# Two-expert-layer kernel behind attention: value products of the odd heads spread over three steps, a one-column bias, gating factors in PSUM, one operand prepared earlier

## The chip, the cores and the metric

One core of one Trainium2 chip. The metric is the device time of one execution in microseconds, the median of several runs. In the text PE is TensorE, DVE is VectorE, ACT is ScalarE, POOL is GpSimd, and SP issues the DMAs.

## What is computed

The reference chains three parts, cut here to what matters.

```python
# attention: batch 2, heads 8, seq 576, head_dim 64, fp32
scores = scale * np.matmul(q, k.transpose(0, 1, 3, 2))
thresh = np.max(scores, axis=-1, keepdims=True) - tau
scores = np.where(scores >= thresh, scores, -1000000000.0)
attn = np.exp(scores - np.max(scores, axis=-1, keepdims=True))
attn = attn / (np.sum(attn, axis=-1, keepdims=True) + 1e-09)
attn_out = np.matmul(attn, v)          # -> x, 1152 x 512
# first expert layer: 8 experts, 512 -> 1024 -> 512
logits = x @ w_gate
P = np.exp(logits - logits.max())
for _ in range(8):
    P /= P.sum(1, keepdims=True) + 1e-09
    P /= P.sum(0, keepdims=True) + 1e-09
    P *= N / E
for e in range(E):
    out += P[:, e:e + 1] * (np.maximum(x @ w1[e], 0.0) @ w2[e])
# second expert layer: the same with 4 experts and p = domain_probs / row sum
```

## The kernel before, in words

**Stage 1, attention, with the first two experts as filling.** The queries of 128 rows by all 576 keys of a head are one unit. The units stand in a list, 72 of them, and `Attention.step` (L388) emits one step per unit as a software pipeline: in step `t` the scores of unit `t+2` are multiplied (`scores`, into one of two PSUM tiles `sc`), unit `t+1` gets its row maximum (`top`, L275), its bias and threshold (`line`, L279) and its exponential (`exp`, L283, on ACT), unit `t` is masked and summed (`mask`, L287, DVE), and normalised on POOL (`norm`, L297), unit `t-2` is transposed on PE (`turn`, L305 and L307) and copied out of PSUM on ACT (`hi`, L312 and L314). Each engine runs its instructions in the order in which they are emitted, so this list of calls sets the order on every queue.

The first 16 units, rows 0 to 255 of batch 0, are the "exact" ones: their probabilities stay in fp32 in one tile `e32` of 5 key blocks by 512 columns, the even head of a pair in columns 0 to 255, the odd head in 256 to 511. Their products with the values (`mix`, L340, written as `pv`) take five key blocks per head, and each block shows as two rows of PE. A group of products (one per head, tied to the head's last unit) is visited in three successive steps: as `c` when that unit is three steps old, as `z` at four, as `y` at five. `parts` (L327) says which of the five blocks are multiplied in which visit, and `out` (L351) splits the finished product into `xh` (ACT, L357) and `xl` (DVE, L358). The other 56 units use a split into high and low fp32r parts, with `lo` (L322, L325) on DVE; from there on PE also gets the work of experts 0 and 1 (`expert_fill`, L460 and L488) between the units. Weights are split into `wh` (ACT) and `wl` (POOL or DVE) as they arrive (`cook`).

`line` makes two numbers of a row's maximum in one DVE instruction on two columns, with a tile `lin` of four columns as its two tensor inputs:

```python
V.scalar_tensor_tensor(st[:, 1:3], lin[:, 0:2], st[:, 0:1], lin[:, 2:4], op0=ALU.mult, op1=ALU.subtract)
```

Column 1 of `st` is the bias of the exponential, column 2 the threshold of the mask.

**Gating.** `gate` (L703) makes the gating matrix `p1` with eight rounds of row and column scaling, on DVE (L731 to L741) with one small product on PE per round (L737, which sums over partitions into a PSUM bank). Row factors `rs` (128x9) and column factors `cs` (128x8) are SBUF tiles. It runs between the last fill work of stage 1. `bank()` hands out PSUM banks, eight at that time.

**Stage 2.** The expert layers are worked off as a list of halves. `layer1` (L842) multiplies seven operand combinations in the order `SLOTS`, each product continuing in a PSUM bank that is copied (`snap`, L890), added to by DVE (L895, L902, L909) and passed through `done` (L860 ACT, L861 DVE); `layer2` (L972) multiplies with the second weights (L989) and accumulates (L997). The operands are sums and differences of `x`, made by `sums` (L761): first DVE sums (L772 to L781), then high and low parts of them by `split` (L71 on ACT, L76 on DVE), three of which live in `xt` (`xth`, `xtl`), six tile parts in all. `sums` is a generator: `s1 = sums(1)` is stopped where it needs `xt`, whose memory comes free only when the fills are closed (L818). After that it is put at the head of the list `behind`, from which `tick` takes one piece at a time, once after each slot of `layer1`; `drain` takes the rest before the first slot that uses `xt` (`u == 6`).

Of the kernel before, what the change touches and what calls it, by code (L numbers as in the profile page):

```python
# [9 lines left out]
F32 = mybir.dt.float32  # L10
F32R = mybir.dt.float32r
AF = mybir.ActivationFunctionType
ALU = mybir.AluOpType
# [3 lines left out]
B, H, S, D = 2, 8, 576, 64  # L17
N, DM, F = 1152, 512, 1024
E1, E2 = 8, 4
P = 128  # L20
KT = DM // P
FT = F // P
NT = N // P
# [6 lines left out]
def attention_two_moe_kernel(ctx, tc, qP, kP, qT, kT, vp, tau, wg, w1, w1s, w2, dp, m2w1s, m2w2, out):  # L30
    nc = tc.nc
    V, A, G, T = nc.vector, nc.scalar, nc.gpsimd, nc.tensor
# [7 lines left out]
    cp = pool(ctx, "const")  # L40
# [14 lines left out]
    warm = cp.tile([P, 1], F32, name="warm")  # L55
    A.activation(warm, ones[:, 0:1], AF.Exp)
    esc = cp.tile([P, 1], F32, name="esc")
    lin = cp.tile([P, 4], F32, name="lin")
    on = cp.tile([P, 1], F32, name="on")
    wg_sb = cp.tile([P, KT, E1], F32, name="wg_sb")  # L60
    wg2 = cp.tile([P, KT, 2 * E1], F32R, name="wg2")
# [49 lines left out]
    class Attention:  # L111
# [164 lines left out]

        def line(self, u):
            st = u["st"]
            V.scalar_tensor_tensor(st[:, 1:3], lin[:, 0:2], st[:, 0:1], lin[:, 2:4], op0=ALU.mult, op1=ALU.subtract)  # L279

        def exp(self, u):
            ex = u["ex"] = self.pl.tile([P, 2, HS], F32, tag="ex", name="ex", bufs=4)
# [43 lines left out]

        def parts(self, hd):  # L327

            return ((0, 1, 2, 3, 4), (), ()) if hd["h"] % 2 else ((0,), (1, 2), (3, 4))

        def mix(self, g, part):
            hd, n, c = g["head"], g["n"], slice(g["c"], g["c"] + g["n"])
# [55 lines left out]
        def step(self, fill, side):  # L388

            us, t = self.units, self.t  # L390
            un = lambda i: us[i] if 0 <= i < len(us) else None
            self.load()
            nxt, a, d, x, c, z, y = (un(t + i) for i in (2, 1, 0, -2, -3, -4, -5))
            if x:
                self.turn(x)
            if d:
                self.mask(d)
            if a:
                self.top(a)
            if d:  # L400
                self.guard(d)
            if a:
                self.line(a)
            if d:
                self.norm(d)
            for part, u in enumerate((c, z, y)):
                for g in u["mix"] if u else ():
                    if g["head"]["exact"]:
                        self.mix(g, part)
            if x:  # L410
                self.hi(x)
            for u, late in ((z, False), (y, True)):
                for g in u["mix"] if u else ():
                    if late == (g["head"]["exact"] and g["head"]["h"] % 2 == 0):
                        self.out(g)
            fill(0, bool(c and c["mix"]))
            if a:
                self.exp(a)
            if x:
                self.lo(x)  # L420
            if nxt:
                self.scores(nxt)
            self.run(self.later)
            for g in c["mix"] if c else ():
                if not g["head"]["exact"]:
                    self.mix(g, 0)
            fill(1, bool(c and c["mix"] or z and z["mix"]))
            self.run(self.late)
            for w in self.work.pop(t, ()):
                w()  # L430
            side()
            self.t += 1
            return self.t < len(us) + 5
# [12 lines left out]
    def bank():  # L446
        return banks.tile([P, 512], F32, tag="mm", name="mm")
# [60 lines left out]
    with ExitStack() as att:  # L508
# [14 lines left out]
        at.plan()  # L523
        room = [2 * FT]
        at.load()
        G.memset(lin, 0.0)
        G.memset(lin[:, 1:2], 1.0)
        V.tensor_scalar(on, tau_sb, 0.0, None, op0=ALU.is_ge)
        V.tensor_scalar(esc, on, 0.125, None, op0=ALU.mult)
        V.tensor_scalar(lin[:, 0:1], on, -0.125, None, op0=ALU.mult)  # L530
        V.tensor_scalar(on, on, -BIG, BIG, op0=ALU.mult, op1=ALU.add)
        V.scalar_tensor_tensor(lin[:, 3:4], tau_sb, 8.0, on, op0=ALU.mult, op1=ALU.add)

        def side():
            if at.t >= -1:
# [140 lines left out]
    behind = []  # L676
# [26 lines left out]
    def gate():  # L703
# [21 lines left out]
        T.matmul(pn[:, 0:1], lhsT=ones[:1, :], rhs=gm[:1, 1:2], start=True, stop=True)  # L725
        V.tensor_scalar(gm[:, 2:3], pn[:, 0:1], -1.0, None, op0=ALU.mult)
        A.activation(p1, p1, AF.Exp, bias=gm[:, 2:3])
        rs = gp.tile([P, NT], F32, name="rs")
        cs = gp.tile([P, E1], F32, name="cs")
        for _ in range(8):  # L730
            V.tensor_reduce(rs, p1, axis=AX.X, op=ALU.add)  # L731
            V.tensor_scalar(rs, rs, 1e-9, None, op0=ALU.add)
# [92 lines left out]
    hp = pool(ctx, "hs", reuse_waits="tile")  # L825
    tp = pool(ctx, "temps", reuse_waits="tile")
    pending = [None, s1]
    behind += [s1, gt, sl]

    def begin(c, work):  # L830
        pending[c] = chain(pending[c] or (), work)
# [240 lines left out]
```

## Time and profile before

| | |
|---|---|
| median of 3 runs | 1394.73 us (1394.54 to 1398.56) |
| the profiled execution's own time | 1393.83 us |
| its span, first to last instruction | 1392.0 us |
| mean granted clock of TensorE over the span | 0.991 |
| POOL busy in the span | 662.0 us (48%) |
| ACT busy in the span | 560.9 us (40%) |

The span is 1.8 us shorter than the execution it belongs to, which holds the start and the end of the program too. A busy share is an average over stages with different limits, so the rows further down are taken stage by stage. In those rows a timeline line gives start, duration, engine, source line, operation, output <- inputs, and in brackets how long the engine sat idle before it and what ended that idle time. A line of a source view gives minimum, median and maximum duration in ns, and the first and last start.

### The profile page before, as it was taken

The page shows a single profiled execution, that of the slowest core. Times are in us where ns is not written, and L with a number is a line of the kernel's source. Part 1 is how long each engine was busy: PE and PEld are TensorE (multiplying, and loading weights), DVE is VectorE, ACT ScalarE, POOL GpSimd, SP SyncE. Part 2 cuts the span into 40 slices and gives each one's busy share as a digit, 9 for nine tenths or more (in the row PEclk, how much of TensorE's full clock was granted, in tenths as well). Part 3 has the DMA queues.
Part 4 walks back from the last instruction along what each step waited for, and adds up shares of the span by engine and source line. Part 5 has one row for each costly group of instructions (what it writes and reads, how often), then busy time and mean ns, then how long its engine had stood idle before and what let it go on. Part 6 is the DMA issues. An engine that isn't in the chain of part 4 may idle for free.

```text
span 1392.0 us, 21443 instructions
## 1 busy us (share of the span) xinstructions
PE 1331.3 (96%) x8089; PEld 1191.5 (86%) x8089; DVE 710.0 (51%) x1579; ACT 560.9 (40%) x1286; POOL 662.0 (48%) x792
## 2 busy tenths in 40 slices
PE   7788999999889999999999999999899999999998
PEld 4578898889779898988889898988788989888887
DVE  6799999555654333343434343435653434334343
ACT  5767677421444242333323242423442424233331
POOL 5766777351565354345335443542433543453330
PEclk9999999999999999999999999999999999999999
DMA  5522231010221111111111011101011101111101
GB/s 164 154 83 78 77 97 44 24 31 9 72 73 54 46 51 34 54 46 31 54 40 60 24 53 47 58 26 46 24 46 46 61 24 54 46 38 47 31 8 61
DMA packets 42055, 73.61 MB, mean 53 GB/s; under 512 B 5088, under 2 KB 10336, under 8 KB 41952
## 3 DMA queue, kind: packets, MB, share of 16 engines
q1 hardware_dynamic: 41664, 71.96, 17.2%
q8 instruction: 64, 1.05, 0.3%
q14 instruction: 39, 0.32, 0.1%
q10 hardware_dynamic: 288, 0.28, 0.1%
HBM read 69.86 MB, written 2.36 MB: 52 GB/s over the span
## 4 chain that ended last, share of the span: by engine, by line
PE 76%; DVE 14%; ACT 5%; issue 2%; POOL 2%; DMA 0%; DVEq 0%; ACTq 0%; POOLq 0%
PE mm L989 37%; PE mm L885 29%; PE mm L488 4%; DVE ex L287 2%; PE mm L460 2%; DVE st L275 2%; DVE st L279 1%; DVE etl L322 1%; DVE mm L895 1%; ACT wh L71 1%; ACT ex L283 1%; PE pv L340 1%; PE sc L270 1%; ACT hs L860 1%; DVE hs L861 1%
## 5 line engine op out<-in xcount | busy, mean ns | idle before, releaser
L989 PE MATMUL mm<-wh,hs 128*128 128x512 f32 x1344 | 433.2, 395 | 0.0
L76 POOL TENSOR_TENSOR wl<-raw,wh 128x512 fp32r<-128x512 f32 x154 | 200.0, 1304 | 396.6 <-ACT wh L71 379.7
L989 PEld LDWEIGHTS mm<-wh,hs 128*128 128x128 f32 x1344 | 252.3, 188 | 58.0 <-DVE hs L861 0.5
L997 DVE SCALAR_TENSOR_TENSOR acc<-mm,p,acc 128x512 f32<-128x512 f32 x181 | 135.7, 750 | 300.9 <-PE mm L989 300.9
L989 PE MATMUL mm<-wl,hs 128*128 128x512 f32 x672 | 264.5, 394 | 0.0
L890 ACT COPY s<-mm 128x288 f32<-128x288 f32 x84 | 33.7, 402 | 439.4 <-PE mm L885 439.3
L885 PE MATMUL mm<-xh,wl 128*128 128x288 f32 x672 | 147.9, 301 | 16.4 <-ACT u L890 14.3
L861 DVE SCALAR_TENSOR_TENSOR hs<-mm,hs 128x288 fp32r<-128x288 f32 x252 | 111.2, 455 | 86.9 <-ACT hs L860 86.9
L860 ACT ACTIVATE hs<-mm 128x288 fp32r<-128x288 f32 x252 | 98.5, 408 | 132.6 <-DVE mm L895 71.8
L989 PEld LDWEIGHTS mm<-wl,hs 128*128 128x128 f32 x672 | 126.4, 188 | 28.2 <-POOL wl L76 0.4
L885 PE MATMUL mm<-xl,wh 128*128 128x288 f32 x672 | 145.0, 297 | 0.0
L885 PE MATMUL mm<-xh,wh 128*128 128x288 f32 x672 | 144.8, 297 | 0.0
L885 PEld LDWEIGHTS mm<-xh,wl 128*128 128x128 f32 x672 | 110.7, 190 | 25.0 <-ACT u L890 15.7
L76 POOL TENSOR_TENSOR wl<-ws,wh 128x512 fp32r<-128x512 f32 x88 | 114.9, 1309 | 32.6 <-ACT wh L71 32.6
L885 PE MATMUL mm<-xth,wl 128*128 128x288 f32 x504 | 109.2, 298 | 1.7 <-ACT xth L71 1.7
L885 PE MATMUL mm<-xtl,wh 128*128 128x288 f32 x504 | 109.2, 298 | 1.5 <-DVE xtl L76 1.5
L885 PEld LDWEIGHTS mm<-xl,wh 128*128 128x128 f32 x672 | 109.0, 190 | 0.0
L885 PE MATMUL mm<-xth,wh 128*128 128x288 f32 x504 | 108.8, 297 | 0.0
L885 PEld LDWEIGHTS mm<-xh,wh 128*128 128x128 f32 x672 | 108.6, 190 | 0.0
L867 POOL TENSOR_SCALAR ht<-hs 128x128 fp32r<-128x128 f32 x168 | 49.7, 302 | 110.5 <-ACT hs L860 97.9
L71 ACT CAST wh<-raw 128x512 fp32r<-128x512 f32 x154 | 95.3, 619 | 2.2 <-DMA raw<-in_w 0.5
L885 PEld LDWEIGHTS mm<-xtl,wh 128*128 128x128 f32 x504 | 81.8, 190 | 2.0 <-DVE xtl L76 2.0
(167 smaller groups left out, 2383.3 us busy)
## 6 DMA issues: line engine op xcount, KB each, us to landing
raw<-in_w SPq DMA_DIRECT2D x88, 256.0 KB, 2.9
raw<-in_w1s SPq DMA_DIRECT2D x56, 256.0 KB, 2.7
raw<-in_m2w1s SPq DMA_DIRECT2D x32, 256.0 KB, 2.7
raw<-in_m2w SPq DMA_DIRECT2D x32, 256.0 KB, 2.9
kr<-in_kT SPq DMA_DIRECT2D x22, 288.0 KB, 2.9
vr<-in_vp SPq DMA_DIRECT2D x24, 160.0 KB, 2.4
qr<-in_qT SPq DMA_DIRECT2D x8, 288.0 KB, 2.8
out_y<-acc SPq DMA_DIRECT2D x8, 256.0 KB, 2.0
```

Of the source, the lines that this page charges most:

```text
L71: A.copy(hi, src)
L76: el.tensor_tensor(lo, src, f(hi), op=ALU.subtract)
L275: V.tensor_reduce(st[:, 0:1], u["sc"][:, :, :HS], axis=AX.XY, op=ALU.max)
L287: V.scalar_tensor_tensor(ex, u["sc"][:, :, :HS], st[:, 2:3], ex, op0=ALU.is_ge, op1=ALU.mult, accum_out=st[:, 3:4])
L488: T.matmul(py[:, :256], lhsT=x, rhs=a[:, c0:c0 + 256], start=i == 0, stop=i == 3 * FT - 1)
L860: A.activation(hh, src, AF.Relu)
L861: V.scalar_tensor_tensor(hl, src, 0.0, f(hh), op0=ALU.max, op1=ALU.subtract)
L867: G.tensor_scalar(tail[j][:, :, q:q + 32], f(side[s][j][:, :, 2 * P:]), 1.0, 1.0, op0=ALU.mult, op1=ALU.mult)
L885: T.matmul(m, lhsT=w[:, (2 * g + kt) * P:(2 * g + kt + 1) * P], rhs=operand(u, kt, lo), start=first and j == 0, stop=j == len(ops) - 1, sk ...
L890: A.copy(z[name], m)
L989: T.matmul(py, lhsT=hs[x][:, k, o:o + P], rhs=w, start=n == 0, stop=n == 3 * HF - 1)
L997: V.scalar_tensor_tensor(acc[t], py, s, acc[t], op0=ALU.mult, op1=ALU.add)
```

## The change

**Value products.** `parts` gave an odd head all five blocks in its first visit; now every exact head but the last one is spread as the even heads were: block 0, then blocks 1 and 2, then 3 and 4. The visits of one step are emitted in the order oldest first (`y`, `z`, `c`) instead of youngest first. The `out` of the odd heads moves to the third visit with it.

**Bias.** `line` becomes two DVE instructions of one column each, with one tensor input (`st`) and a per-partition scalar (`lin`, now two columns). Two POOL memsets of `lin` go.

**Gating factors.** `rs` and `cs` become slices of one PSUM bank, held as long as the gating runs.

**Operand preparation.** The rest of `s1` is emitted at once, ahead of the first `layer1`, instead of standing first in `behind`.

```diff
-    lin = cp.tile([P, 4], F32, name="lin")
+    lin = cp.tile([P, 2], F32, name="lin")
...
-            V.scalar_tensor_tensor(st[:, 1:3], lin[:, 0:2], st[:, 0:1], lin[:, 2:4], op0=ALU.mult, op1=ALU.subtract)
+            V.tensor_scalar(st[:, 1:2], st[:, 0:1], lin[:, 0:1], None, op0=ALU.mult)
+            V.tensor_scalar(st[:, 2:3], st[:, 0:1], lin[:, 1:2], None, op0=ALU.subtract)
...
-            return ((0, 1, 2, 3, 4), (), ()) if hd["h"] % 2 else ((0,), (1, 2), (3, 4))
+            return ((0, 1, 2, 3, 4), (), ()) if hd["h"] == H - 1 else ((0,), (1, 2), (3, 4))
...
-            for part, u in enumerate((c, z, y)):
+            for part, u in ((2, y), (1, z), (0, c)):
...
-                    if late == (g["head"]["exact"] and g["head"]["h"] % 2 == 0):
+                    if late == (g["head"]["exact"] and g["head"]["h"] < H - 1):
...
-        G.memset(lin, 0.0)
-        G.memset(lin[:, 1:2], 1.0)
...
-        rs = gp.tile([P, NT], F32, name="rs")
-        cs = gp.tile([P, E1], F32, name="cs")
+
+        norms = bank()
+        rs, cs = norms[:, :NT], norms[:, 16:16 + E1]
...
-    behind += [s1, gt, sl]
+    for _ in s1:
+        pass
+    behind += [gt, sl]
```

PE's queue in the exact stage, from the step in which the first odd head has its first visit, before (`pv` are the value products, `sc` the scores, `et` and `er` the transposes; L340 is `mix`):

```order
L307 MATMUL er<-ident,ex 64x128
L340 MATMUL pv<-e_125,vr 64x256 x7
L270 MATMUL sc<-kh,qs 128x288 x2
L270 MATMUL sc<-kl,qs 128x288 x2
L305 MATMUL et<-ident,ex 128x128 x4
L307 MATMUL er<-ident,ex 64x128
L270 MATMUL sc<-kh,qs 128x288 x2
L270 MATMUL sc<-kl,qs 128x288 x2
L305 MATMUL et<-ident,ex 128x128 x4
L307 MATMUL er<-ident,ex 64x128
L340 MATMUL pv<-e_125,vr 64x256
```

The same piece now (the lines of the file moved by one):

```order
L308 MATMUL er<-ident,ex 64x128
L341 MATMUL pv<-e_125,vr 64x256 x3
L270 MATMUL sc<-kh,qs 128x288 x2
L270 MATMUL sc<-kl,qs 128x288 x2
L306 MATMUL et<-ident,ex 128x128 x4
L308 MATMUL er<-ident,ex 64x128
L341 MATMUL pv<-e_125,vr 64x256 x2
L270 MATMUL sc<-kh,qs 128x288 x2
L270 MATMUL sc<-kl,qs 128x288 x2
L306 MATMUL et<-ident,ex 128x128 x4
L308 MATMUL er<-ident,ex 64x128
L341 MATMUL pv<-e_125,vr 64x256 x3
```

The blocks per step go from 7, 0, 1, 2 to 3, 2, 3, 2 (one row of this list is one block), and in the steps with three the two of the older head stand first.

ACT's queue where stage 2 begins, before (`acc` is the last copy of the fills, `s` and `u` are snaps of `layer1`, `xth` the six casts of the rest of `s1`, `wh` a weight):

```order
L493 COPY acc_3656<-mm 128x256 x2
L890 COPY s<-mm 128x288
L71 CAST xth<-xy 128x288
L890 COPY s<-mm 128x288
L71 CAST wh<-raw 128x512
L71 CAST xth<-xy 128x288
L860 ACTIVATE hs<-mm 128x288
L71 CAST xth<-xy 128x288
L860 ACTIVATE hs<-mm 128x288
L71 CAST wh<-raw 128x512
L71 CAST xth<-xy 128x288 x3
L890 COPY u<-mm 128x288 x2
```

And now:

```order
L494 COPY acc_3726<-mm 128x256 x2
L71 CAST xth<-xy 128x288 x6
L892 COPY s<-mm 128x288 x2
L71 CAST wh<-raw 128x512
L862 ACTIVATE hs<-mm 128x288 x2
L71 CAST wh<-raw 128x512
L892 COPY u<-mm 128x288 x2
```

The six casts moved ahead of the first snap, and on DVE the six `xtl` (L76) ahead of the first L895; PE's own order is unchanged there.

## Rows read from the trace of the kernel before

**Rows 1.** The page: busy time, share of the span and instructions of each engine.

```profile
PE 1331.3 (96%) x8089; PEld 1191.5 (86%) x8089; DVE 710.0 (51%) x1579; ACT 560.9 (40%) x1286; POOL 662.0 (48%) x792
```

**Rows 2.** Busy time by stretch: stretch, its length, busy time (instructions) of PE, PEld, DVE, ACT, POOL, then the granted TensorE clock, the DMA share and GB/s. The stretches are the exact units, the split units, the fills after them, the gating, the start of stage 2 and the steady part of stage 2.

```profile
28.00:77.00 49.00, 38.46 (x207) 23.85 (x205) 36.52 (x98) 34.02 (x66) 34.63 (x37) 1.00 0.49 141
77.00:228.00 151.00, 138.67 (x1046) 131.45 (x1044) 143.12 (x363) 110.48 (x215) 108.25 (x147) 0.99 0.28 81
228.00:293.00 65.00, 62.63 (x485) 60.12 (x484) 34.65 (x92) 30.38 (x68) 29.93 (x58) 1.00 0.08 25
293.00:313.00 20.00, 17.62 (x144) 17.07 (x144) 18.41 (x48) 5.88 (x14) 11.81 (x9) 1.00 0.11 27
352.00:372.00 20.00, 16.74 (x103) 15.26 (x103) 10.33 (x21) 10.76 (x28) 8.13 (x8) 0.91 0.19 59
480.00:1392.00 912.00, 896.32 (x5177) 800.84 (x5175) 372.94 (x748) 306.34 (x757) 380.95 (x413) 1.00 0.14 42
```

**Rows 3.** What PE waited for in 28 to 77 us: who waited for whom, us in total, times, longest.

```profile
PE sc L270 <- DVE ex L287: 9.1, 9, 1.4
PE et L305 <- DVE etl L322: 1.4, 2, 1.1
```

**Rows 4.** What ACT waited for in the same stretch, same columns.

```profile
ACT e L312 <- PE pv L340: 6.8, 3, 3.1
ACT ex L283 <- DVE st L295: 5.9, 7, 1.1
```

**Rows 5.** Timeline of the exact stage: the three copies `e` that waited for `pv`, one burst of `pv`, one step with two blocks of `pv`, and a wait of the scores.

```profile
31.61 0.59 ACT L312 COPY e<-et 128x512 f32<-128x512 f32 x1 [3.11 <-PE pv L340]
...
42.41 3.66 PE L340 MATMUL pv<-e,vr 128*64 128x256 f32 x14
...
45.59 0.59 ACT L312 COPY e<-et 128x512 f32<-128x512 f32 x1 [2.09 <-PE pv L340]
...
48.64 0.54 PE L270 MATMUL sc<-kh,qs 128*128 128x288 f32 x2 [1.31 <-DVE ex L287]
...
52.91 1.08 PE L340 MATMUL pv<-e,vr 128*64 128x256 f32 x4
...
59.44 0.59 ACT L312 COPY e<-et 128x512 f32<-128x512 f32 x1 [1.58 <-PE pv L340]
```

**Rows 6.** What PE waited for in 77 to 228 us, the longest in total (us in total, times, longest).

```profile
PE et L305 <- DVE etl L322: 10.3, 13, 1.9
```

**Rows 7.** The chain of work that ended last, shares of the stretch 77 to 228 us by line.

```profile
by line: DVE ex L287 16.6%; DVE st L275 14.2%; DVE st L279 11.8%; DVE etl L322 11.0%; PE mm L488 6.8%; DVE eth L325 4.6%; ACT ex L283 4.5%; DVE xf L369 4.3%; DVE hl L469 4.3%; issue 4.1%; POOL wl L98 2.4%; PE et L305 1.7%; POOL xl L76 1.6%;
```

**Rows 8.** Three DVE lines over the whole span: `line` (L279), the guard of the sum (L291) and the mask (L287), minimum, median and maximum ns.

```profile
L279 DVE SCALAR_TENSOR_TENSOR st<-lin,st x72: 220/472/1323, 6.9 to 251.8; 128x2 f32<-128x2 f32 x72
...
L291 DVE TENSOR_SCALAR st<-st x72: 133/143/154, 9.5 to 253.9; 128x1 f32<-128x1 f32 x72
...
L287 DVE SCALAR_TENSOR_TENSOR ex<-sc,st,ex x72: 799/817/820, 8.1 to 253.0; 128x576 f32<-128x576 f32 x72
```

**Rows 9.** Busy time of L279 alone in the exact and the split stretch (stretch, length, DVE busy and instructions, clock, DMA).

```profile
28.00:77.00 49.00, 7.39 (x14) 1.00 0.49 141
77.00:228.00 151.00, 24.34 (x43) 0.99 0.28 81
```

**Rows 10.** Timeline of DVE and POOL at two units: L291 and L279 with POOL idle, then POOL's `kl` and the L279 beside it.

```profile
41.67 0.14 DVE L291 TENSOR_SCALAR st<-st 128x1 f32<-128x1 f32 x1
41.79 0.22 DVE L279 SCALAR_TENSOR_TENSOR st<-lin,st 128x2 f32<-128x2 f32 x1
...
44.20 1.40 POOL L76 TENSOR_TENSOR kl<-kr,kh 128x576 fp32r<-128x576 f32 x1
...
44.50 1.11 DVE L279 SCALAR_TENSOR_TENSOR st<-lin,st 128x2 f32<-128x2 f32 x1
```

**Rows 11.** The DVE lines of the gating, minimum, median and maximum ns of the eight rounds.

```profile
L732 DVE TENSOR_SCALAR rs<-rs x8: 173/174/896, 293.3 to 327.0; 128x9 f32<-128x9 f32 x8
...
L734 DVE TENSOR_TENSOR p<-p,rs x8: 232/234/1129, 294.4 to 327.5; 128x72 f32<-128x72 f32 x8
...
L741 DVE SCALAR_TENSOR_TENSOR p<-p,cs x8: 232/232/971, 297.0 to 332.0; 128x72 f32<-128x72 f32 x8
...
L731 DVE TENSOR_REDUCE rs<-p x8: 229/229/231, 293.0 to 326.8; 128x9 f32<-128x72 f32 x8
...
L738 DVE TENSOR_REDUCE cs<-mm x8: 215/222/232, 296.2 to 331.3; 128x8 f32<-128x72 f32 x8
```

**Rows 12.** Timeline where stage 2 begins: ACT's last copy of the fills, the three matmuls that waited, and the later casts of `sums(0)`, six in a row.

```profile
352.97 0.37 ACT L493 COPY acc<-mm 128x256 f32<-128x256 f32 x1 [2.45 <-PE mm L488]
...
357.23 0.40 PE L885 MATMUL mm<-xtl,wh 128*128 128x288 f32 x1 [0.70 <-DVE xtl L76]
...
360.55 0.40 PE L885 MATMUL mm<-xth,wl 128*128 128x288 f32 x1 [1.74 <-ACT xth L71]
...
361.89 0.61 PE L885 MATMUL mm<-xtl,wh 128*128 128x288 f32 x1 [0.81 <-DVE xtl L76]
...
384.09 2.10 ACT L71 CAST xth<-xy 128x288 fp32r<-128x288 f32 x6
```

**Rows 13.** The same columns as rows 2, for 3.2 us behind those waits and 3.2 us before them; both hold matmuls of the same size.

```profile
361.80:365.00 3.20, 3.11 (x13) 3.11 (x14) 0.81 (x4) 0.88 (x2) 1.35 (x1) 0.53 0.08 16
352.80:356.00 3.20, 3.20 (x27) 3.20 (x26) 1.10 (x3) 2.36 (x6) 0.43 (x1) 1.00 0.18 65
```

More of the change, by code (lines that the diff above doesn't have):

```diff
@@ L531, in attention_two_moe_kernel @@
         V.tensor_scalar(on, on, -BIG, BIG, op0=ALU.mult, op1=ALU.add)
-        V.scalar_tensor_tensor(lin[:, 3:4], tau_sb, 8.0, on, op0=ALU.mult, op1=ALU.add)
+        V.scalar_tensor_tensor(lin[:, 1:2], tau_sb, 8.0, on, op0=ALU.mult, op1=ALU.add)
         def side():
```

## The prediction

> **What bounds the kernel now.** First the page: PE is busy 96% of the span and, its own weight loads (PEld) apart, nothing else over 51% [rows 1], so the kernel is a PE kernel, and what can be had is the time in which PE stands. The table by stretch says where that is [rows 2]. From 480 us to the end PE stands 15.7 us in 912 and the change touches nothing there; between 228 and 293 us it stands 2.4. Four places are left: 28 to 77 us (49 - 38.46 = 10.5 us of standing), 77 to 228 (151 - 138.67 = 12.3), the gating from 293 to 313 (2.4) and the start of stage 2 from 352 to 372 (3.3). Everything behind the last place is PE work at 98%, which gives nothing back: what PE gains earlier should reach the end.
>
> Then who ends the standing. In the exact units it is the mask on DVE, 9.1 us in nine waits [rows 3], and behind DVE stands ACT: its copies `e` waited 6.8 us for the value products, its exponentials 5.9 us for the step on DVE that makes their bias [rows 4]. In the split units 10.3 us of PE's waits are for `etl` on DVE [rows 6], and the chain there is DVE almost throughout, L279 with 11.8% of it [rows 7], though that instruction handles two columns. Its duration shows why: 220 ns at best, 472 at the median, 1323 at worst [rows 8]. Beside an idle POOL it took 0.22 us; begun while POOL's `kl` ran from 44.20 to 45.60, it took 1.11 and ended as that did [rows 10]. L291, one column wide, between the same neighbours, never left 133 to 154 ns in 72 instances [rows 8].
>
> **The change part by part.**
>
> *Bias.* One L279 goes per unit, two one-column instructions come. Their price I take from L291: 0.14 us each, 0.12 from one start to the next [rows 8, 10], so 0.24 per unit on DVE, and 0.14 until the bias is there. In the split stretch L279 holds 11.8% of 151 us, 17.8 us of the chain [rows 7]; at a mean of 24.34 / 43 = 0.57 us [rows 9], less some 0.08 by which neighbours overlap, these are about 36 of the 43 units. The pairs put back 36 x 0.24 = 8.6, so 9.2 go. PE stands 12.3 there, but in some units it is as full as DVE and regains nothing: I take 8 (bounds 4 and 9.2). In the exact stretch the seven waits of the exponential each shrink by about 7.39 / 14 - 0.14 = 0.39 [rows 4, 9]: 2.7 us. The other 15 units lie before 28 us or behind 228; for them I take 0.5, between 0 and 1. The two POOL memsets gone stand ahead of anything POOL is waited for: nothing.
>
> The one-column form with a per-partition scalar is not in the trace. Below, a pair cannot beat 2 x 0.12; above, each could wait as L279 does. I take L291's price since that is the same operation in the same tile and size, and because L287, which reads a per-partition scalar beside an SBUF tensor, stays within 799 to 820 ns [rows 8].
>
> *Value products.* A burst of seven blocks is 14 rows of PE in 3.66 us, two blocks are 4 rows in 1.08 [rows 5], so the ten rows of the odd head take 2.58. ACT's next copy `e` overwrites columns that the even head's last two blocks still read, and these stood last in the burst. Now they stand first, and the copy may start up to 2.58 us earlier: of its waits of 3.11, 2.09 and 1.58 us [rows 5] go 2.6 + 2.1 + 1.6 = 6.3. The burst of the last pair stays. The eight rows that leave a burst land in the two next steps, four in each, 1.03 us: there PE waited for the mask 1.0 us on average, 1.31 in the case shown [rows 3, 5]. That wait is the cover; gone, the six steps would cost up to 6.2 and eat the gain. `xh` and `xl` of the odd heads come a step later, and nobody reads them before the fills. Together with the bias 9.0 us could go of the 10.5 that PE stands. I take 6.5: over 42.5 instead of 49 us ACT (34.0) and POOL (34.6) would be busy 80% [rows 2], and queues that run in order do not pack tighter for free. Bounds 3 and 9.
>
> *Gating.* DVE is busy 18.4 of 20 us in the stretch [rows 2], and three lines of a round swell while POOL works: L732 from 0.17 to 0.90, L734 from 0.23 to 1.13, L741 from 0.23 to 0.97 [rows 11]. With the factors in PSUM each has at most one SBUF tensor. PE's 2.4 us of standing is all there is; I take 2 (bounds 0 and 2.4). Reading PSUM costs no more on such sizes: L738 reads it in 222 ns, L731 reads SBUF in 229 [rows 11]. The bank held leaves seven to hand out; PE's order is the same.
>
> [...]
>
> *Operand preparation.* PE waited 0.70 + 1.74 + 0.81 = 3.25 us for the pieces of `s1` [rows 12]. [...] Now the six casts run in a row from ACT's last copy at 352.97 + 0.37 on, in 2.1 us as later ones did [rows 12], so the last is done at 355.4, before PE reaches the slot that needs them at about 356. Against it: `s` and `u` come 1.5 to 2 us later on ACT, and the product that continues behind `u` may wait up to 0.9 (an estimate: PE comes there seven slots of six matmuls on, at 3.2 / 27 us each [rows 13], 5 us, ACT after the casts, two copies, two weights and two activations, 6 us). 3.25 + 1.7 - 0.9 = 4.0; bounds 2 and 4.9.
>
> **Sum.** 8 + 0.5 + 6.5 + 2 + 4 = 21 us. The sum is made against the profiled execution: 1393.8 - 21 = 1372.8, and the median of the runs lies 0.9 above it, within their spread. I predict 1373.
>
> **Rivals.**
>
> *The cover is too short.* In the exact units the moved products displace scores that are waited for, or POOL's queue (35 of 49 us busy, with three kinds of work that PE waits for) sets the pace; in the split units PE, already at 92%, takes DVE's place [rows 2]. At the lower bounds 4 + 0 + 3 + 1 + 2 = 10 us: 1384. For it speaks that rarely every wait on a chain goes at once; against it, that most of PE's standing in both stretches is for DVE alone [rows 3, 6].
>
> *Every wait goes.* At the upper bounds 9.2 + 1 + 9 + 2.4 + 4.9 = 26.5: 1367.
>
> *L279 is long for another reason than its two tensor inputs*, so that the change does not shorten it: the burst, gating and `s1` are left without the bias, some 4 + 0 + 4 = 8 us: 1386. The rows of L291 and L279 side by side speak against it.
>
> *Slower: the one-column instructions wait for POOL too, each for itself.* The place is `line` in all units. L732 shows it, a one-tensor instruction from SBUF to SBUF that grew to 896 ns [rows 11]. L279 is 0.57 - 0.22 = 0.35 above its undisturbed value in the split units; if POOL starts its next work between the two, a pair takes 2 x (0.12 + 0.35) = 0.94 against 0.49 now, 0.45 x 36 = 16 us more there, and 0.45 x 7 = 3 in the exact units; less 6.3 for the bursts, 2 and 4, that is 7 us more: 1401. It decides from a mean of about 0.4 us per new instruction. Against it, 72 rows of L291 at most 154 ns [rows 8], with POOL busy 108 of 151 us [rows 2]. [...]
>
> **How the numbers follow.** The forecast 0.65 (its own range 1368 to 1379), cover too short 0.20, every wait 0.07, L279 unchanged 0.05, slower 0.03. The range from 1365 to 1385 leaves out the slower case, most of the unchanged one and the tails of the others, under 2 in 10. A measurement of this kernel tells about 0.3%, 4.2 us, from no change. Faster by more is every case but the slower one and the poorest of the second and fourth: 0.92; within 0.3%: 0.05; slower: 0.03.
>
> **What would show it.** In the profile after: no DVE instruction of `line` above 0.2 us and the chain between 77 and 228 us without it; the exact units done some 6 us and the split units some 14 us earlier; no copy `e` that waits over 1.1 us for `pv` ahead of the last pair; PE without a wait for `xth` or `xtl` at the start of stage 2 and the clock at 1.00 there. It would be wrong if the new instructions follow POOL's work in length, if PE's waits for `sc` turn into waits for POOL, or if a later stretch than the fourth grows by what the earlier ones gave.

## The result, and the profile after

The changed kernel takes 1372.71 us (median of 4 runs, 1372.41 to 1374.51), the kernel before 1395.01 (4 runs, 1394.54 to 1398.56): 22.3 us faster. The ratio, taken from all runs and not from the two medians, is 0.9837 with a 95% interval from 0.9819 to 0.9856, which is 22.7 us. The kernel before has one run more here than in the table ahead of the prediction. The forecast was 1373, with a range from 1365 to 1385. The profiled execution of the changed kernel took 1374.51 us, its span 1372.6, against 1393.83 and 1392.0 before. Two executions of the experiments, 1854.53 us of the kernel before and 1912.65 of a_two_inputs, ran at mean clocks of 0.65 and 0.63, and the ratios leave them out.

The page, part 1, as in [rows 1]:

```profile
PE 1328.1 (97%) x8089; PEld 1189.9 (87%) x8089; DVE 693.1 (50%) x1651; ACT 559.0 (41%) x1286; POOL 660.7 (48%) x790
```

About the same places of the program as in [rows 2], without the fills after the split units (exact units, split units, gating, start of stage 2, steady part; columns as there). The first row starts about half a microsecond early; the last two lie between the same matmuls as before:

```profile
27.40:71.40 44.00, 40.61 (x212) 24.93 (x212) 34.91 (x112) 34.62 (x68) 35.49 (x37) 0.98 0.54 159
71.40:216.40 145.00, 137.01 (x1046) 131.73 (x1045) 133.95 (x406) 109.26 (x215) 107.88 (x147) 0.99 0.29 85
281.30:298.60 17.30, 17.18 (x144) 16.98 (x143) 15.09 (x49) 5.88 (x14) 11.73 (x9) 1.00 0.11 31
337.60:353.30 15.70, 15.06 (x104) 13.89 (x102) 8.41 (x21) 10.65 (x28) 8.10 (x8) 1.00 0.23 75
461.70:1372.60 910.90, 895.23 (x5176) 800.41 (x5174) 373.33 (x748) 305.72 (x757) 380.00 (x413) 1.00 0.14 42
```

PE stands 3.4 us in the exact units (10.5 before), 8.0 in the split ones (12.3), 0.1 in the gating (2.4), 0.6 at the start of stage 2 (3.3), and 15.7 in the steady part as before. The two lines of `line`, the guard (now L292) and the gating's lines, minimum, median and maximum ns; they answer [rows 8, 11]:

```profile
L279 DVE TENSOR_SCALAR st<-st,lin x72: 211/214/216, 6.8 to 239.8; 128x1 f32<-128x1 f32 x72
...
L280 DVE TENSOR_SCALAR st<-st,lin x72: 201/204/207, 7.0 to 239.9; 128x1 f32<-128x1 f32 x72
...
L292 DVE TENSOR_SCALAR st<-st x72: 132/144/153, 9.4 to 241.8; 128x1 f32<-128x1 f32 x72
...
L732 DVE TENSOR_SCALAR mm<-mm x8: 174/175/175, 281.5 to 312.6; 128x9 f32<-128x9 f32 x8
...
L734 DVE TENSOR_TENSOR p<-p,mm x8: 228/228/230, 282.0 to 313.1; 128x72 f32<-128x72 f32 x8
...
L741 DVE SCALAR_TENSOR_TENSOR p<-p,mm x8: 228/228/229, 285.2 to 317.6; 128x72 f32<-128x72 f32 x8
...
L731 DVE TENSOR_REDUCE mm<-p x8: 235/236/236, 281.3 to 312.3; 128x9 f32<-128x72 f32 x8
...
L738 DVE TENSOR_REDUCE mm<-mm x8: 222/230/242, 284.5 to 316.8; 128x8 f32<-128x72 f32 x8
```

No instance waits for POOL any more: minimum and maximum lie within 21 ns. Then the waits in the exact units (27.4 to 71.4), who for whom, us, times, longest, beside [rows 3, 4]:

```profile
ACT ex L284 <- DVE st L279: 4.2, 7, 1.2
...
PE sc L270 <- DVE ex L288: 2.2, 4, 0.7
...
PE et L306 <- DVE etl L323: 1.2, 2, 0.9
...
ACT e L313 <- PE pv L341: 1.1, 1, 1.1
```

PE's waits for the mask went from 9.1 to 2.2 us, ACT's for `pv` from 6.8 to 1.1. In the split units PE's wait for `etl` went from 10.3 to:

```profile
PE et L306 <- DVE etl L323: 5.2, 7, 1.0
```

and in the chain there PE's lines now stand first, L279 has 2.2% where it had 11.8 [rows 7]:

```profile
by line: PE mm L461 11.6%; PE mm L489 11.0%; DVE ex L288 9.2%; DVE st L275 7.9%; PE sc L270 7.3%; issue 7.2%; PE et L306 6.7%; PE pv L350 4.6%; PE pv L348 4.1%; ACT ex L284 4.0%; DVE etl L323 3.8%; POOL ex L298 2.5%; DVE st L279 2.2%; DVE h
```

At the start of stage 2 the timeline has the six casts in one row, and one short wait where three stood [rows 12]; the clock there is 1.00 (fourth line of the table above):

```profile
338.77 2.11 ACT L71 CAST xth<-xy 128x288 fp32r<-128x288 f32 x6
...
339.31 2.30 DVE L76 TENSOR_TENSOR xtl<-xy,xth 128x288 fp32r<-128x288 f32 x6
...
344.59 0.53 PE L887 MATMUL mm<-xh,wl 128*128 128x288 f32 x2 [0.56 <-ACT u L892]
```

### The profile page after: what moved, and what is told of

It is laid out like the page before. It is cut to its first block, busy times and chain, and to the rows that moved or that the text cites. A ratio compares the mean times of both kernels' runs of the same rounds, so it can differ in the third digit from the quotient of the medians.

```text
span 1372.6 us, 21582 instructions
## 1 busy us (share of the span) xinstructions
PE 1328.1 (97%) x8089; PEld 1189.9 (87%) x8089; DVE 693.1 (50%) x1651; ACT 559.0 (41%) x1286; POOL 660.7 (48%) x790
## 4 chain that ended last, share of the span: by engine, by line
PE 80%; DVE 11%; ACT 5%; issue 2%; POOL 1%; DMA 0%; DVEq 0%; ACTq 0%; POOLq 0%
PE mm L991 37%; PE mm L887 29%; PE mm L489 5%; PE mm L461 3%; DVE ex L288 2%; PE sc L270 1%; DVE st L275 1%; DVE mm L897 1%; PE et L306 1%; ACT wh L71 1%; ACT hs L862 1%; ACT ex L284 1%; DVE hs L863 1%; PE pv L350 1%; PE pv L348 1%
## 5 line engine op out<-in xcount | busy, mean ns | idle before, releaser
L76 POOL TENSOR_TENSOR wl<-raw,wh 128x512 fp32r<-128x512 f32 x154 | 199.7, 1301 | 390.4 <-ACT wh L71 374.0
L76 POOL TENSOR_TENSOR wl<-ws,wh 128x512 fp32r<-128x512 f32 x88 | 114.1, 1300 | 32.8 <-ACT wh L71 32.8
L625 POOL TENSOR_TENSOR ws<-raw 128x512 f32<-128x512 f32 x44 | 57.4, 1304 | 54.4 <-DMA raw<-in_w1s 32.1
```

What stands on the lines that cost most here:

```text
L76: el.tensor_tensor(lo, src, f(hi), op=ALU.subtract)
L625: G.tensor_tensor(s, a, b, op=op)
```

## The experiments

Where the time went is read at five marks that every kernel has: the start of the mask in units 0, 20 and 71 (units are counted from 0), the start of the last scaling of `acc` by the gating (L753 of the kernel before), and the end of the span. The table gives by how much each stretch is shorter than in the kernel before (us, each from one profile, so the place of a drop of the clock is in it), and the ratio of the timed runs to those of the kernel before on the same chip. Beside the experiments these had medians from 1395.0 to 1396.7 us on three chips, so times of different chips are compared by the ratios; 0.1% is 1.4 us. Names with b_ are the kernel before with one edit, those with a_ the changed kernel with one.

| kernel | ratio (95%) | units 0 to 20 | 20 to 71 | to the last scaling | stage 2 |
|---|---|---|---|---|---|
| changed | 0.9837 (0.9819 to 0.9856) | 5.7 | 6.4 | 2.4 | 4.9 |
| b_bias | 0.9952 (0.9936 to 0.9968) | 3.0 | 6.3 | -0.8 | -2.6 |
| b_values | 0.9976 (0.9964 to 0.9988) | 4.5 | -1.1 | -2.9 | -2.2 |
| b_gating | 0.9975 (0.9965 to 0.9984) | 0.0 | 0.1 | 2.6 | -1.7 |
| b_s1 | 0.9969 (0.9958 to 0.9981) | 0.0 | -0.2 | -1.4 | 3.8 |
| b_order | 0.9990 (0.9978 to 1.0001) | 1.4 | 1.4 | -1.5 | -0.9 |
| b_spread | 0.9976 (0.9964 to 0.9988) | 3.2 | -0.1 | 0.0 | -0.6 |
| a_two_inputs | 0.9969 (0.9956 to 0.9983) | 0.8 | -6.8 | 2.6 | 4.6 |
| a_two_columns | 0.9932 (0.9918 to 0.9945) | 1.3 | -0.5 | 2.6 | 4.4 |
| a_one_column | 0.9872 (0.9854 to 0.9891) | 4.3 | 5.8 | 1.2 | 4.0 |
| a_sbuf_gating | 0.9867 (0.9846 to 0.9888) | 6.8 | 7.7 | -0.3 | 3.8 |
| a_no_guard | 0.9830 (0.9813 to 0.9846) | 6.8 | 7.8 | 2.6 | 4.8 |
| a_act_no_guard | 0.9827 (0.9811 to 0.9844) | 6.8 | 7.3 | 2.8 | 4.3 |

**The four parts alone.** Each is its piece of the diff on the kernel before. *b_bias:* 

> The kernel before with the bias part alone: two one-column instructions for L279, lin in two columns, no memsets. Theory (the long L279 is its two tensor inputs beside POOL, and it stood on the path): 7 to 8 us faster, as the trace of the changed kernel gained 6.4 us between units 20 and 63 and some 0.9 us in the exact units; no line instruction above 0.25 us. If the bursts of value products hid the long L279 in the exact units, the gain is that of the split units alone, 6.4. Rival (L279 is long because DVE is held at that place, whatever stands there): the new instructions are long, or the ones behind them, and the time is within 1 us of before.

*b_values:* 

> The kernel before with the value products alone: odd heads spread over three steps, older heads first. Theory (the copy e behind a burst comes free earlier, and each of three bursts was a delay of its own): 4.6 us faster, the sum of what the three bursts gave in the changed kernel (1.47 + 1.55 + 1.57), whatever the bias does. Rival (the bias had to be short first: behind a shorter burst ACT and PE wait for the long L279 instead, so that burst and L279 hide each other): 2 to 3 us alone, and more than 7.5 us would then be missing from the sum of the single parts.

*b_gating:* 

> The kernel before with the gating factors in PSUM alone. Theory (lines with one SBUF tensor no longer wait for POOL): 2.7 us faster, as the changed kernel gained between the start of the gating and its last round, and no instruction of the gating above 0.25 us. Rival (the rounds became short only because POOL's work fell elsewhere in time, after the other parts): the lines stay long in some rounds and the gain is under 1 us. [...]

*b_s1:* 

> The kernel before with the operand preparation alone, the rest of s1 ahead of the first layer1. Theory (three waits of 0.70 + 1.74 + 0.81 us and 1.7 us of half clock behind them go, 0.6 us of a wait for u comes): 4 to 5 us faster, clock 1.00 behind the start of stage 2. Rival (the half clock is not tied to those waits): 2.5 us faster, and the clock still falls there.

By the ratios the time falls by 0.48, 0.24, 0.25 and 0.31%, that is 6.7, 3.3, 3.5 and 4.3 us, within 2.2, 1.7, 1.3 and 1.6; for the bias 7 to 8 were expected. Each part gains in its own stretch: 3.0 and 6.3 (bias), 4.5 (values), 2.6 (gating), 3.8 (s1). For the bias in the split units, the gating and s1 the theory holds and the rivals don't: no instruction of `line` takes over 217 ns in b_bias, no DVE instruction of the gating's rounds over 242 in b_gating, and in b_s1 the clock is 1.00 from 350 to 370 us. In the exact units less is settled. The profiles of b_bias and b_values show a clock of 1.00 from 20 to 30 us, where the kernel before has 0.83 on the mean: by estimate up to 10 x 0.17 = 1.7 us that the edits need not have earned. That leaves 1.3 to 3.0 for the bias and 2.8 to 4.5 for the values, against the 0.9 and 4.6 expected, and for the values the rival's 2 to 3 is not excluded. The bursts do not hide the long L279 altogether, but how far the two hide each other stays open. The four add up to 1.28%, 17.9 us, where the whole gives 1.63%, 22.7 us; the difference, 0.35% or 4.9 us, is just outside its uncertainty of 4.3. The negative entries show part of it: without the other parts, later stretches took up to 2.9 us longer than in the one profile of the kernel before. At the start of stage 2 the reason is visible, a drop of the clock. Two windows of b_bias behind the waits for `xth` and `xtl` (columns as in rows 2):

```profile
350.00:355.00 5.00, 2.45 (x12) 1.99 (x11) 3.32 (x7) 3.03 (x8) 2.31 (x2) 0.76 0.00 2
355.00:360.00 5.00, 5.00 (x25) 5.00 (x24) 1.37 (x3) 1.90 (x5) 1.59 (x2) 0.56 0.15 52
```

The mean granted clock over these 10 us is 0.66, by estimate a loss of up to 10 x 0.34 = 3.4 us. In the kernel before the same 10 us read:

```profile
358.40:363.40 5.00, 2.44 (x12) 1.99 (x11) 3.31 (x7) 3.03 (x8) 2.32 (x2) 0.80 0.00 2
363.40:368.40 5.00, 5.00 (x35) 5.00 (x34) 1.83 (x4) 2.83 (x7) 1.75 (x3) 0.86 0.17 52
```

0.83 on the mean, up to 1.7 us, as in b_order and b_spread. In b_values and b_gating it is 0.66 and 3.4 again: the profile on which the prediction rests had the smaller of the two sizes that this drop takes in these profiles.

In the gating the reason is POOL again. With the factors in SBUF the eight rounds took 39.2 us in the kernel before, b_order and b_spread, where six instructions waited for POOL (0.88 us and more each), but 39.7, 40.7 and 40.6 in b_bias, b_values and b_s1, where seven did: 0.5 + 1.4 + 1.4 = 3.3 us that three of the single parts lost there, by one profile each, and a large part of the 4.9. With the factors in PSUM none waited, and the rounds took 36.3 to 36.7 us in b_gating and the six kernels of the table that keep this part. Why POOL's work met one instruction more in those three stays open. Over all profiles of the table and the one before, stage 2 is 5.7 us shorter with the early operands (mean of eight, +4.3) than without (mean of six, -1.3).

**Order against spreading.** The two edits of the value products one by one:

```diff
# b_order
-for part, u in enumerate((c, z, y)):
+for part, u in ((2, y), (1, z), (0, c)):
# b_spread
-return ((0, 1, 2, 3, 4), (), ()) if hd["h"] % 2 else ((0,), (1, 2), (3, 4))
+return ((0, 1, 2, 3, 4), (), ()) if hd["h"] == H - 1 else ((0,), (1, 2), (3, 4))
...
-if late == (g["head"]["exact"] and g["head"]["h"] % 2 == 0):
+if late == (g["head"]["exact"] and g["head"]["h"] < H - 1):
```

> The kernel before with the order of the visits alone: older heads first, bursts of seven blocks kept. Theory (the copy e waits only for the last two blocks of the even head, which now stand first): its waits of 3.1, 2.1 and 1.6 us fall by 2.6, 2.1 and 1.6, and the exact units are done nearly as much earlier as with both edits, 3.5 to 4.5 us by unit 20. Rival (PE itself is the delay, the burst of 3.66 us stands in front of the next scores): the waits of e go, but scores and masks come no earlier, under 1.5 us.

> The kernel before with the odd heads spread over three steps, but the youngest head first as it was. Theory (the place of the even head's last two blocks decides, and they now stand behind one or two blocks instead of five): e still waits 0.5 to 1 us longer than with both edits, 2.5 to 4 us earlier by unit 20. Rival (the burst in front of the next scores is the delay): 4.4 us by unit 20, the same as both edits together.

Order alone gives 1.4 us by unit 20, where the rival said under 1.5; spreading alone gives 3.2, within the theory's 2.5 to 4; both together 4.5. The clock is in these figures: b_order's profile has two drops more in the exact units than the kernel before (0.86 on the mean from 30 to 40 us, 0.83 from 50 to 60), b_values's one less. Up to the mask of unit 8, behind the first burst, b_order, b_spread and the kernel before have had the same one drop (0.83 from 20 to 30 us), and there the order gives 0.6 us and the spreading 2.6. In b_order, waits of 28 to 77 us:

```profile
PE sc L270 <- DVE ex L287: 4.8, 4, 1.7
ACT e L312 <- PE et L305: 4.5, 3, 1.7
...
ACT e L312 <- PE pv L340: 1.2, 2, 0.7
```

and its timeline at the first burst, PE and the copies `e`:

```profile
28.55 3.66 PE L340 MATMUL pv<-e,vr 128*64 128x256 f32 x14
29.24 0.58 ACT L312 COPY e<-et 128x512 f32<-128x512 f32 x1 [0.67 <-PE pv L340]
...
32.15 0.54 PE L270 MATMUL sc<-kh,qs 128*128 128x288 f32 x2
...
32.79 0.60 PE L305 MATMUL et<-ident,ex 128*128 128x128 f32 x4
...
33.42 0.59 ACT L312 COPY e<-et 128x512 f32<-128x512 f32 x1 [1.70 <-PE et L305]
```

The first copy comes 2.4 us earlier than in [rows 5], of the 2.6 expected, but the next one now waits for transposes that stand behind the whole burst on PE. In b_spread the copies wait for `pv` as little as in b_order (6.8 us before):

```profile
ACT e L312 <- PE pv L340: 1.2, 1, 1.2
```

So the burst delayed in two ways, by holding `e32` and by standing in front of the next scores and transposes. Either edit nearly ends the first, and only spreading ends the second, which is the larger. The size of b_spread came out as expected, but not for the reason given there.

**What makes `line` wait for POOL.** Three forms of it on the changed kernel, with `lin` back in four columns:

```diff
-V.tensor_scalar(st[:, 1:2], st[:, 0:1], lin[:, 0:1], None, op0=ALU.mult)
-V.tensor_scalar(st[:, 2:3], st[:, 0:1], lin[:, 1:2], None, op0=ALU.subtract)
# a_two_inputs: one column, two tensors
+V.scalar_tensor_tensor(st[:, 1:2], lin[:, 0:1], st[:, 0:1], lin[:, 2:3], op0=ALU.mult, op1=ALU.subtract)
+V.scalar_tensor_tensor(st[:, 2:3], lin[:, 1:2], st[:, 0:1], lin[:, 3:4], op0=ALU.mult, op1=ALU.subtract)
# a_two_columns: two columns, one tensor
+V.tensor_scalar(st[:, 1:3], lin[:, 0:2], st[:, 0:1], lin[:, 3:4], op0=ALU.mult, op1=ALU.subtract)
# a_one_column: the operands of a_two_columns, a column at a time
+V.tensor_scalar(st[:, 1:2], lin[:, 0:1], st[:, 0:1], lin[:, 3:4], op0=ALU.mult, op1=ALU.subtract)
+V.tensor_scalar(st[:, 2:3], lin[:, 1:2], st[:, 0:1], lin[:, 3:4], op0=ALU.mult, op1=ALU.subtract)
```

> The changed kernel with its two one-column instructions of line written as the old operation, each with a second one-column tensor from SBUF (lin back in four columns). Theory (what makes the instruction wait for POOL is the second SBUF tensor input, not the width): they grow to 0.9 us and more where POOL works, some of the pairs twice, and the time is 7 to 15 us above the changed kernel, 1380 to 1388. Rival (it was the two columns): no instruction of line above 0.25 us and the time of the changed kernel within 2 us.

> The changed kernel with line as one instruction of two columns and one tensor input (lin), its other two operands per-partition scalars; bias and threshold are both lowered by the threshold's offset, which cancels in the normalised row. Theory (the second tensor input alone makes the wait): every line instruction stays near 0.21 us; DVE has 0.13 us a unit less, 5.6 in the 43 split units, of which none to half reaches the end: 0 to 3 us faster than the changed kernel. Rival (an instruction with one SBUF tensor in and out of SBUF waits for POOL too as soon as it is wider than one column, as the 128x9 line of the gating did): up to 1 us long, some 6 to 9 us slower than the changed kernel, the whole bias term gone.

> The changed kernel with line as two one-column instructions that have the operands of the two-column one: a column of lin as the only tensor, the row's maximum and the threshold's offset as per-partition scalars, two operations each. Theory now (an instruction from SBUF to SBUF escapes POOL only with one tensor input and one column): no line instruction above 0.3 us in 144, some 0.29 each, and the time within 3 us of the changed kernel, 1372 to 1376. Rival (the operands of the two-column one made the wait, its two scalars or lin as the tensor, and not the second column): up to 1.1 us long, 1385 or more.

The instructions of `line` in a_two_inputs (1392.16 us):

```profile
L279 DVE SCALAR_TENSOR_TENSOR st<-lin,st x72: 219/350/1362, 6.8 to 257.8; 128x1 f32<-128x1 f32 x72
...
L280 DVE SCALAR_TENSOR_TENSOR st<-lin,st x72: 204/209/1330, 6.9 to 257.9; 128x1 f32<-128x1 f32 x72
```

in a_two_columns (1385.81 us):

```profile
L279 DVE TENSOR_SCALAR st<-lin,st x72: 286/474/1312, 6.9 to 251.1; 128x2 f32<-128x2 f32 x72
```

and in a_one_column (1378.72 us):

```profile
L279 DVE TENSOR_SCALAR st<-lin,st x72: 272/273/278, 6.9 to 241.9; 128x1 f32<-128x1 f32 x72
...
L280 DVE TENSOR_SCALAR st<-lin,st x72: 261/266/268, 7.1 to 242.1; 128x1 f32<-128x1 f32 x72
```

Either is enough in these operations: a second tensor from SBUF (up to 1362 ns), or a second column (up to 1312). My theory held for the first, though the loss (1.3%, 18 us, against the changed kernel) is larger than the 7 to 15 expected. It fell for the second, where the rival was right in kind and too low in size (13 us, where it said 6 to 9, with one instruction less). Of these forms only one tensor and one column escapes (278 ns at most). a_two_inputs also shows the mechanism of the slower rival, both instructions of a pair waiting, one for each piece of POOL's work, though in 3 of the 72 pairs only (37 others have one that takes over 0.3 us, nearly always the first); its DVE timeline

```profile
56.48 0.51 DVE L279 SCALAR_TENSOR_TENSOR st<-lin,st 128x1 f32<-128x1 f32 x1
56.92 1.30 DVE L280 SCALAR_TENSOR_TENSOR st<-lin,st 128x1 f32<-128x1 f32 x1
```

and POOL's beside it:

```profile
55.56 1.42 POOL L76 TENSOR_TENSOR kl<-kr,kh 128x576 fp32r<-128x576 f32 x1 [0.52 <-ACT kh L71]
56.94 1.26 POOL L98 TENSOR_TENSOR wl<-raw,wh 128x512 fp32r<-128x512 f32 x1
```

a_one_column has the operands of a_two_columns and does not wait (278 ns at most against 1312), so it is the width. But its time lies 6.0 us above the changed kernel (0.35%, 4.9 us, by the ratios), where at most 3 were expected. Its second scalar, with the second operation, makes each instruction 0.06 longer (273 and 266 ns at the median against 214 and 204) and the pair 0.37 from its start to the reciprocal's instead of 0.25, 72 x 0.12 = 9 us of DVE; I had not priced that. It is not shown that all of the loss comes from there: of the 4.3 us between the two spans 2.0 lie in the units (3.3 if units 20 to 71 are set against a_sbuf_gating's, which kept the clock at 1.00 from 130 to 150 us as this one did), and the rest behind them, where `line` does not run.

Tensors and width are not all that decides here, for the operation counts too. In the rounds of the gating of the kernel before, the reciprocal has one tensor of nine columns, from SBUF to SBUF, and never left 215 to 217 ns, where the TENSOR_SCALAR ahead of it (L732), on the same nine columns, took up to 896 [rows 11]. DVE in one round, and POOL beside it:

```profile
298.22 0.90 DVE L732 TENSOR_SCALAR rs<-rs 128x9 f32<-128x9 f32 x1
299.15 0.21 DVE L733 RECIPROCAL rs<-rs 128x9 f32<-128x9 f32 x1
299.40 1.02 DVE L734 TENSOR_TENSOR p<-p,rs 128x72 f32<-128x72 f32 x1
```

```profile
297.79 1.30 POOL L76 TENSOR_TENSOR wl<-ws,wh 128x512 fp32r<-128x512 f32 x1
299.05 1.28 POOL L76 TENSOR_TENSOR wl<-raw,wh 128x512 fp32r<-128x512 f32 x1
```

The reciprocal begins and ends inside POOL's second piece; the instructions around it end within 0.1 us of the ends of the first and the second.

**The gating's factors back in SBUF**, on the changed kernel:

```diff
-norms = bank()
-rs, cs = norms[:, :NT], norms[:, 16:16 + E1]
+rs = gp.tile([P, NT], F32, name="rs")
+cs = gp.tile([P, E1], F32, name="cs")
```

> The changed kernel with the gating factors back in SBUF tiles. Theory (the parts add up): 2.7 us slower, what PSUM gave in the gating of both kernels. Rival (how the gating's rounds meet POOL's work is a matter of the moment at which it starts; the kernel before met it well, and the three kernels with another part alone lost 0.8, 2.9 and 1.4 us there): 3.5 to 5.5 us slower, single lines up to 1.3 us, and this is a part of what the single parts' sum lacks.

The same three lines swell to the values of [rows 11], six instructions in all, and the stretch to the last scaling loses 2.4 + 0.3 = 2.7 us: the theory, by the trace. The ratios differ by more, 0.30% or 4.2 us, with an uncertainty of 3.9. This does not decide between the two. That the rounds can meet POOL worse is seen in b_bias, b_values and b_s1 (in b_bias the instruction that adds 1e-9 to `cs` took up to 1324 ns), not here.

**One step on.** DVE was still busy 134 of 145 us in the split units, so I took instructions from it.

```diff
# a_no_guard
-            if d:
-                self.guard(d)
...
-V.reciprocal(st[:, 5:6], st[:, 4:5])
+V.reciprocal(st[:, 5:6], st[:, 3:4])
# a_act_no_guard, besides
-V.tensor_scalar(st[:, 2:3], st[:, 0:1], lin[:, 1:2], None, op0=ALU.subtract)
+A.activation(st[:, 2:3], st[:, 0:1], AF.Identity, bias=lin[:, 1:2])   # ahead of the exponential; lin[:, 1] negated
```

> The changed kernel without the guard instruction: the row sum holds an exponential of zero, so it is at least 1, and 1e-9 more is the same number in fp32. Theory (DVE still sets the pace in the attention units, busy 134 of 145 us in the split ones): the guard's 0.12 us from start to start go in 72 units, 8.6 us of DVE, of which some six in ten reach the end as with the bias: 4 to 5 us faster than the changed kernel. Rival (PE, now at 137 of 145 us, has taken DVE's place): under 1.5 us.

> As the one without guard, and the threshold moved to ACT, one Identity activation with a per-partition bias ahead of the exponential, so that DVE has one line instruction left. Theory (DVE sets the pace): another 0.13 us a unit of DVE, 3 to 4 us more, 7 to 9 us faster than the changed kernel together. Rival (ACT is next: 72 activations of some 0.2 us stand ahead of exponentials for which DVE waits): no gain over the one without guard, or a loss of up to 5 us.

1372.61 and 1372.41 us, ratios of 0.9830 and 0.9827 beside 0.9837: neither can be told from the changed kernel. By the number that is what the two rivals said. But for the guard both the theory and the rival are beside the point. DVE at one unit, in the changed kernel

```profile
127.91 0.75 DVE L275 TENSOR_REDUCE st<-sc 128x1 f32<-128x576 f32 x1
128.57 0.14 DVE L292 TENSOR_SCALAR st<-st 128x1 f32<-128x1 f32 x1
128.69 0.21 DVE L279 TENSOR_SCALAR st<-st,lin 128x1 f32<-128x1 f32 x1
```

and without the guard:

```profile
127.69 0.75 DVE L275 TENSOR_REDUCE st<-sc 128x1 f32<-128x576 f32 x1
128.47 0.21 DVE L279 TENSOR_SCALAR st<-st,lin 128x1 f32<-128x1 f32 x1
```

L279 starts 0.78 us behind the start of the maximum in both, and 0.77 to 0.80 in all 72 units of either kernel. It reads what L275 writes, and taking the guard out did not bring it forward; the guard ran in the gap, for nothing. In the units a_no_guard gains 6.8 and 7.8 us, a_sbuf_gating, with the guard and the same clock, 6.8 and 7.7. With the threshold on ACT, DVE does get lighter, but not PE. The split units of a_act_no_guard (columns as in rows 2):

```profile
71.40:216.40 145.00, 136.48 (x1054) 131.31 (x1053) 129.37 (x324) 117.60 (x259) 108.76 (x148) 1.00 0.29 85
```

DVE 4.6 us less, ACT 8.3 more (the one-column activation took 0.28 to 0.31 us, not the 0.2 expected), and PE stands 8.5 us, not less than the 8.0 of the changed kernel. Its largest wait there, `etl`, shrank from 5.2 to 2.6, and waits for POOL took its place (3.6 us, 0.5 in the changed kernel). The chain there is now PE's own work for the most part:

```profile
by line: PE mm L488 15.0%; PE mm L460 14.9%; PE sc L270 11.4%; PE et L307 9.0%; PE pv L351 6.2%; issue 5.8%; PE pv L349 5.5%; DVE ex L289 3.9%; DMA vr<-in_vp 3.1%; ACT ex L285 3.0%; DVE st L275 2.8%; POOL qs L240 2.6%; POOL ex L299 2.6%; PE
```

The six PE lines hold 62% of it, 45% in the changed kernel, and DVE's mask and maximum 7% where they had 17%. By the chain DVE no longer sets the pace there; whether more of PE's remaining waits can go was not tried.

## Why the prediction was right, point by point

**What bounds the kernel: right.** PE's busy time hardly moved (1331.3 to 1328.1), its standing went in the four places named, and what they gave reached the end: 5.7 + 6.4 + 2.4 + 4.9 = 19.4 us between the two spans.

**Sum: 21 forecast, 22.3 between the medians, 19.4 between the two profiled executions.** The one of after was the slowest of its four: its clock from 20 to 30 us was 0.66 on the mean, 0.83 before, by estimate up to 10 x 0.17 = 1.7 us. a_sbuf_gating, the same code up to the gating, stood at 0.83 there, kept 1.00 from 130 to 150 us, where both others dropped for a while (0.85 and 0.83 over ten us), and had 6.8 and 7.7 in the first two stretches. One of the prediction's sums has a slip: its first rival takes 1 for the gating where the lower bound was 0, so the lower bounds give 9 us, 1385, and not 10.

**Bias, 8 in the split units: 6.4, or 7.7 in that other profile, units 20 to 71 together.** The price was right by luck in one half. From L279 to the reciprocal a pair takes 0.25 us, 0.24 was assumed; but each instruction takes 0.21 and 0.20, not L291's 0.14: at the median 214 and 204 ns with a per-partition scalar against 144 with the immediate of L292, 0.06 to 0.07 more. Bounds 4 to 9.2 held. *The reason was half of it.* I wrote that L279 is long for its second tensor and set aside the width; the runs show that a second column suffices. The new form escapes as L291 does (216 ns at most, L291 154), and matches it in both.

The slower rival rested on L732, one tensor and nine columns, and was in that better than I took it: with one tensor, two columns waited (up to 1312 ns in a_two_columns), though one column did not (216 at most in the changed kernel). At one column, two tensors from SBUF waited beside POOL's work, up to 1362 ns in a_two_inputs.

**Exact stage, 6.5: 5.7, or 6.8.** The size held, the step for the value products only in part. The waits of `e` went as worked out (6.8 to 1.1), but by b_order they were the smaller part of the gain (0.6 us at the first burst, 1.4 by unit 20), not 6.3; the rest is the burst's place ahead of the next transposes and scores, which the prediction did not name. So the size is luck in part. The cover, PE's wait for the mask, held: 2.2 us of 9.1 are left, and 5.9 in b_values. The bias gave 3.0 here by itself, at least 1.3 without the clock (2.7 was forecast).

**Gating, 2: 2.4, and 2.6 and 2.7 in two experiments.** Nearly all of PE's standing there went. The factors in PSUM cost the two reductions 7 to 8 ns (L731 236 against 229, L738 230 against 222) and the two reciprocals 12 to 13 (L733 227 against 215, L740 216 against 203); the other lines differ by 6 at most.

**Operand preparation, 4.0: 4.9, and 5.7 as the mean of profiles, above the bound of 4.9.** The 1.7 in the prediction's sum is an estimate from [rows 13]: 13 matmuls in 3.2 us at a granted clock of 0.53 where 27 ran at 1.00, 3.2 x (1 - 13/27). This half clock is the mis-sized term: 1.7 us in the profile read, by estimate up to 3.4 in three of the five others that kept the waits (a mean clock of 0.66 over ten us against 0.83). The mean holds all else that differs in stage 2 too. The new wait for `u` was 0.56, 0.9 was allowed.

**Tell-tales.** `line` stayed at 0.216 us at most, not quite under 0.2, and has 2.2% of the chain, not none; the exact units came 5.7 us earlier (some 6), the split units 12.0 (some 14, so 2 short); no `e` waits over 1.1; no wait for `xth` or `xtl`, clock 1.00. Of what would have made it wrong nothing came.

## What to carry to other kernels

`line`, a small VectorE instruction that took 472 ns at the median and 220 at its minimum [rows 8], was waiting, and not working: compare such an instruction with its neighbours by number of SBUF tensors, by width and by operation, and test each alone, since here each of them made a difference (1362 ns at worst with a second tensor, 1312 with a second column, 217 for the RECIPROCAL of nine columns). Before a short instruction is taken off a busy engine, look whether it stands between a producer and its reader; there it can be free, as the guard was, with L279 some 0.78 us behind the start of L275 with it and without it. A clock drop read from one profile is one sample (a mean of 0.83 over ten us in three profiles behind the same stall, 0.66 in three others), and the cost of a stall with such a drop behind it should be given a bound from more than one.

## What was not expected of the hardware

- With POOL working, a VectorE instruction from SBUF to SBUF waited with two columns and one tensor (286 ns at best, 1312 at worst, TENSOR_SCALAR, a_two_columns) and with one column and two tensors (219 and 1362, SCALAR_TENSOR_TENSOR, a_two_inputs), but not with one and one (211 and 216, TENSOR_SCALAR, the changed kernel). A RECIPROCAL with nine columns and one tensor did not wait (215 to 217, the kernel before).
- A one-column TENSOR_SCALAR took 0.144 us at the median with an immediate, 0.214 with one per-partition scalar (both in the changed kernel), and 0.273 with two and a second operation (a_one_column): about 0.07 us for the first scalar, 0.06 for the second with its operation.
- The reader of the 128x576 maximum started 0.77 to 0.80 us behind the maximum's start on VectorE, with an independent instruction of 0.14 us between them (the changed kernel) or without it (a_no_guard).
- The drop of the clock behind the same stall at the start of stage 2 had two sizes: the mean over the ten us there was 0.83 in three of the profiles that have the stall (the kernel before, b_order, b_spread), and 0.66 in the other three (b_bias, b_values, b_gating).
